# Gating the first weight loads on the second piece of x, with a new order of loads and new lists, in a fused attention and two-layer kernel

## The chip, the core and the metric

The kernel runs on one NeuronCore of a Trainium2 chip. The metric is the device time of one execution in microseconds (us); lower is better. Engines are named as in the profile: PE (TensorE, with PEld for its weight loads), DVE (VectorE), ACT (ScalarE), POOL (GpSimd) and SP (SyncE).

## The reference

Shapes: `x` is 8 batches x 8 heads x 512 tokens x 64, `state` is 8 x 8 x 32 x 64, `w_in` is 512 x 2048, `w_out` is 2048 x 512, `s` and `b` are single numbers. All are float32.

```python
# attention, per batch and head, scale = 1/8
a     = softmax(scale * x @ state.T)        # 512 x 32
xread = a @ state                           # 512 x 64
a2    = softmax(scale * state @ x.T)        # 32 x 512
sread = a2 @ x                              # 32 x 64
rows  = concat([xread, sread], axis=tokens) # 544 tokens a batch, 512 wide over the heads
# two layers on all 4352 rows
h = rows @ w_in
g = s * relu(h) ** 2 + b
out = g @ w_out
```

## The kernel before, in words

**Tiling.** The 512 tokens of a batch are one unit of work, and the eight batches go through the same steps. For a batch, `x` is transposed (`xT`), the scores of all heads come out as one tile of 128 partitions (8 heads x 32 states in two groups `g`) by 512 tokens (`T`, then `E` after the exponential, which also leaves the row sums for `sread`), and the softmax over the 32 states divides by column sums that a matmul with a block matrix of ones makes (`D`, then a logarithm and an exponential of its negative on ACT, then a product on DVE: `a4`). The read of the states and the first layer are folded together: `M[b, c] = state x w_in` for the quarter `c` of the 2048 columns (`part_M`, 8 small matmuls on quarters of the array), so that the first layer is `M.T @ a4` (`layer1`, 32 matmuls of 512 columns a batch, two groups accumulated). ACT takes the relu out of PSUM (line 996), DVE squares it (line 1002). The second layer of batch 0 is 64 plain matmuls of 512 columns (`layer2_first`); later batches use sums and differences of blocks (`pair_sums`, `weight_sums`, `layer2`) with 256 columns. The 32 rows of `sread` of all batches are done last (`layer1_slots`, `layer2("sr")`).

**PSUM.** There are three pairs of banks (`ps`, traced as `pair`) and two single banks (`ob`, traced as `o`). A product `M[b, c]` named in `APART` is written to two single banks, one per group, and copied by two instructions that may be on two engines; another is written to one pair and copied whole (batch 0's `c` of 0 and 1 by two copies out of the pair).

**The order of the work.** Every step is an `op` with its reads and writes. `TURNS` gives, for each engine, the numbers of its steps in the order in which that engine issues them; `Plan.order` merges the five lists and chooses buffers. An engine therefore never passes a step whose inputs are late: what stands behind it waits. In the first 20 us `Plan.order` also puts in matmuls on a tile of zeros (`fill`, traced as `warm`) where PE would otherwise sit idle; there are 59 of them.

**The loads at the start.** SP issues the four pieces of batch 0's `x` (`x0_load`, tile `xf`, traced as `u`, two heads of each half of the heads in each) and two tiny loads of `s` and `b`. ACT issues the identity and the first batch's states (`stf[0]`). GpSimd issues the loads that also turn float32 into float16: the quarters of `w_in` (`wi`, from 1 MB each to 512 KB), the quarters of `w_out` (`wo`) and the batches of `x` (`xn`). All of these wait for one small copy on GpSimd, the *gate* (line 552), which reads two columns of the identity, so no load of this queue is issued before the identity has landed. The order of GpSimd's loads is: gate, `wi0`, the states of batches 1 and 2 (`stf[1]`), `x` of batch 1, `wi1`, `wo0`, `wi2`, `wo1`, `wi3`, `wo2`, `wo3`, `x` of batch 2 and so on. A load that would be the ninth on its way waits for the one eight before it.

**The states.** `st_v` reads `state` with a state's 64 numbers (256 bytes) as one piece. `att_st(i)` casts them, each doubled, to `st16` (DVE), transposes them on PE with `is_transpose` into float16 in PSUM and copies them to `stT` (DVE).

Of the kernel before, what the change touches and what calls it, by code (L numbers as in the profile page):

```python
# [11 lines left out]
FP16 = mybir.dt.float16  # L12
# [6 lines left out]
        27 29 25 31 35 33 39 36 40 50 48 80-81 187 84-85 185 53 59 189 92-93 88-89 117 192 118 125-126 121  # L19
        113 122-123 127 119 68 70 114-115 124 116 128 193 120 96 141 129-130 99 237 131-133 225 74 134 142  # L20
        135 145 136 234 137 146 102 147 105 149 148 150-152 161-162 76 108 165-166 240 163 138 111 143
        167-168 164 243 139 222 144 72 62 157 140 158 153 159 56 228 154 160 231 173 155 174 1051 65 330 175
        156 169-171 267 333 258 334 259 268 260-263 269-270 172 176 271 264 272-274 348 351 1056 78 265 345
        354 360 286 277 287-289 694 445 278-281 290-291 282-284 339 357 292 342 293 295-299 454 567 1061
        305-306 300-301 307 302 308 696 576 452 309 315 310 316 311 317 312 318-322 570 572 1066 375-379 448
        689 450 384-387 380 476 388 381-382 467 479 464 389-390 394 482 395 461 391 470 396-397 403 398-401
        473 592 404-405 412 406-407 413-415 408-409 416 410 589 417-419 422 698 692 574 432-436 583 437
        423-424 438 425 439 426-428 586 429 604 601 506 497 507 711 595 498-499 508 598 509 500 510 501-504
        511-512 714 513 516-519 1071 1076 525-526 520-521 527 522-523 528 939 811 529-530 534 531-532
        535-541 544 820 932 935 554-556 545 557-561 546 720 723 619-621 726 622 547-549 705 550-551 623-626  # L30
        717 708 628-630 638-639 631-633 640 634-635 641-642 848 647 643 648-653 644-645 654 845 656-663 1086
        1081 937 941 666-668 676-677 669-670 814 816 818 671-672 678-680 673 954 681 836 741-744 682-683 830
        745-746 957 747 750 748 751-753 833 754-755 760 756 761-763 757 764-766 842 769-770 767 771-775
        778-781 776 782-785 839 788 798-799 789 800 790 801 827 969 963 791 802-805 951 960 1106 792 863 948
        864 793 865 794 866 795 867 1101 868-870 872-878 1091 882 879 883 966 884-888 891-892 1096 889
        893-898 900-906 910 907 911-915 920-921 916-917 1121 1111 984 922 1116 985-986 923 987 924-926
        988-989 927 990 1126 993 991 994-1000 1003-1010 1012-1019 1021-1028 1031-1035 1041 1036 1042
        1037-1038 1043-1048 1143-1150 1152-1159 1162-1169 1171-1178 1180-1187 1190-1197 1200-1207
    """,
    "ACT": """  # L40
        20-21 30 23 37 41 38 42 44 52 45 51 82 86 60 190-191 94 90 194-195 69 197-198 97 100 238 226 235 103
        106 77 109 241 244 223 63 57 229 232 67 331-332 335-336 349 352 79 346 361 355 695 447 446 340 358
# [4 lines left out]
    """,  # L47
    "DVE": """
        24 28 22 26 34 32 6 47 43 49 46 188 83 186 61 7 87 54-55 1057 91 71 95 196 199 98 75 1052 214 101
        239 210 104 215 206 236 107 207 227 110 252 112 218 209 179 177 64 73 245 58 219 242 224 1053 233 66  # L50
        220 230 246 216 253 325 337 183 208 181 247 1058 211 266 248 275 249 347 255 250 256-257 350 356 212
        217 213 285 221 1062 353 254 251 1067 294 341 457 1063 458 303 459 344 369 313 323 1068 363 370 364
        362 359 366 579 371 367 580 365 383 372 581 368 373 392 466 701 402 374 472 1072 484 463 478 469 411
        702 420 481 1077 485 703 475 491 440 585 430 494 594 488 495 492 489 486 588 487 606-608 713 505 597
        514 603 1078 496 493 616 524 940 490 533 1073 542 591 1082 610 936 562 823-824 600 825 944 552 613
        627 1087 617 722 611 945 614 719 636 609 946 728 716 646 615 612 655 707 618 1088 664 1083 942 725
        735 819 710 674 729 684 738 732-733 956 749 730 850 736 739 737 847 758 835 731 768 777 786 734 832
        838 854 740 841 860-861 844 971 959 806 829 855 857 1110 796 851 965 858 852 859 871 962 1105 880
        953 975 856 950 853 972 890 968 1108 899 1103 908 862 976-977 918 1100 981 1098 978 1118 973 1113
        982 928 983 992 979 1125 974 1001 1093 1120 980 1011 1128 1130 1095 1131 1020 1134 1123 1115 1135  # L60
        1029 1137 1140 1136 1138 1132 1141 1039 1049 1151 1160 1133 1142 1170 1139 1179 1188 1198 1208
    """,
    "POOL": """
        8-9 11 16 10 12-15 17-19 329 200 204 202 444 566 180 304 314 276 393 688 810 1060 421 441 182 431
        515 563 324 184 665 178 637 675 1065 1055 759 1070 1080 543 1075 1090 1085 807 685 909 881 919 553
        787 929 797
    """,
    "SP": """
        0-5 327 201 203 328 442 205 443 326 564 338 565 456 1059 687 686 578 460 1064 700 582 1054 704 930
        808-809 931 1079 822 943 1074 826 947 1084 1069 1089 1050 1040 1030 1161 1002 1189 1199 1209  # L70
# [16 lines left out]
class Plan:  # L87
# [60 lines left out]
    def order(self, fill):  # L148
# [3 lines left out]
        dma_free = {"sw": 7.05, "hw": 0.0}  # L152
# [5 lines left out]
        mode, out = "full", []  # L158
# [138 lines left out]
def kernel(  # L297
# [18 lines left out]
    P = 128  # L316
# [36 lines left out]
    APART = {(1, 0), (1, 1), (2, 0), (2, 1)}  # L353
# [40 lines left out]

    nc.vector.memset(warm, 0.0)
# [43 lines left out]
    def x0_load(i):  # L439
        op(  # L440
            {"SP": 0.5},
            lambda e: nc.sync.dma_start(xf_ap(i), x0_v[:, x0_heads(i)]),
            wr=[K(("xf", i))],
            dma=("hw", 0.75),
            lands=(3.6, 4.7, 6.0, 6.5)[i],
        )
# [25 lines left out]
    def wi_load(c):  # L472
        op(
            {"POOL": 0.85},
            lambda e: nc.gpsimd.dma_start(
                out=wi[c],
                in_=moe_w_in.rearrange("(k p) f -> p k f", p=P)[:, :, c * FC : c * FC + FC],
            ),
            rd=[g0],
            wr=[K(("wi", c))],  # L480
            dma=("sw", MB),
        )
# [61 lines left out]
    for i in range(4):  # L544
# [14 lines left out]
    op(  # L559
        {"POOL": 0.9},  # L560
# [858 lines left out]
```

## Time and profile before

| what | value |
|---|---|
| median of 3 runs | 208.2 us (207.3 to 208.93) |
| the profiled execution's own time | 208.01 us |
| its span, first to last instruction | 206.2 us |
| PE busy, PE matmuls | 199.3 us (97%), 1989 |
| DVE, ACT, POOL busy | 164.3, 109.3 and 38.8 us |
| granted clock of PE | 1.000 |
| HBM read, written | 17.33 MB, 8.91 MB |

The execution takes 1.8 us more than its span. A "busy" PE counts the zero-tile matmuls too, and overlapping matmuls are shown with more than their share (a 512-column matmul has 379 ns in its row, while the next one begins 216 ns later), so the work that PE has got done by a moment is counted in matmuls, not in busy time. `wi` and `wo` appear as sources by those names, the gate as `gate`, the identity as `ident`, the states as `stf`, `st` and `stT`.

### The profile page before, as it was taken

The numbers are of one execution on the slowest core, as the hardware profiler recorded it, in microseconds if no ns is written. First come the engines' busy times: TensorE is split into PE (matmuls) and PEld (weight loads), VectorE is DVE, ScalarE is ACT, GpSimd is POOL, SyncE is SP. The second block draws the span as 40 slices with busy tenths as digits, with TensorE's granted clock in tenths as the row PEclk, the third lists the DMA queues.
The fourth block names the chain that finished last, engine by engine and source line by source line (L and its number), as shares of the span: only waits on it lengthen the run. The fifth ranks groups of instructions, "written<-read, shape, count | busy, mean of one in ns | idle before, by whom it ended". The sixth has DMA issues, their size and how long they took to land.

```text
span 206.2 us, 4768 instructions
## 1 busy us (share of the span) xinstructions
PE 199.3 (97%) x1989; PEld 134.7 (65%) x1989; DVE 164.3 (80%) x325; ACT 109.3 (53%) x153; POOL 38.8 (19%) x60
## 2 busy tenths in 40 slices
PE   7979999999999999999999999999999999999992
PEld 3744444435666665677577767766776688888881
DVE  2327637989899979899999988997969689859871
ACT  4757786467588879468644473254606634130000
POOL 4832002001020120331301030033070200331000
PEclk9999999999999999999999999999999999999999
DMA  5999999992999992798991470233020200253054
GB/s 173 201 197 204 206 205 179 179 198 16 186 139 195 143 221 41 110 134 154 199 194 60 80 222 13 51 111 118 0 103 3 102 0 2 71 187 105 0 176 131
DMA packets 47285, 25.83 MB, mean 125 GB/s; under 512 B 31616, under 2 KB 45440, under 8 KB 47264
## 3 DMA queue, kind: packets, MB, share of 16 engines
q0 software_dynamic: 13792, 15.34, 38.0%
q1 hardware_dynamic: 33056, 10.10, 26.4%
q8 instruction: 15, 0.25, 0.5%
q10 hardware_dynamic: 416, 0.10, 0.2%
q14 instruction: 6, 0.05, 0.1%
HBM read 17.33 MB, written 8.91 MB: 127 GB/s over the span
## 4 chain that ended last, share of the span: by engine, by line
PE 89%; DMA 7%; DVE 1%; issue 0%; ACT 0%; POOL 0%; DVEq 0%
PE o L335 48%; PE pair L335 41%; DMA wi<-in_moe_w_in_dram 4%; DMA out_dram<-osb 2%; DMA ident<-ident_const 1%; DVE osb L1281 0%; DVE M L422 0%; ACT M L422 0%; DVE osb L1270 0%; DVE aN L906 0%; DVE sr L933 0%; POOL gate L552 0%; DVEq L1270 0%
## 5 line engine op out<-in xcount | busy, mean ns | idle before, releaser
L996 ACT ACTIVATE g<-pair 128x1024 f16<-128x1024 f32 x64 | 63.0, 1023 | 44.5 <-PE pair L335 44.4
L335 PE MATMUL pair<-a,M 128*128 128x512 f16 x256 | 63.3, 379 | 0.1
L335 PEld LDWEIGHTS <-pd 128*128 128x128 f16 x480 | 46.4, 98 | 10.1 <-issue 1.5
L335 PEld LDWEIGHTS <-g 128*128 128x128 f16 x424 | 40.7, 98 | 17.5 <-issue 2.9
L1002 DVE TENSOR_TENSOR g<-g 128x1024 f16<-128x1024 f16 x64 | 42.8, 683 | 2.8 <-ACT g L996 2.8
L335 PE MATMUL o<-u,pd 128*128 128x256 f16 x360 | 44.2, 273 | 0.0
L335 PE MATMUL o<-wo,g 128*128 128x256 f16 (+1 forms) x272 | 42.6, 285 | 0.0
L335 PEld LDWEIGHTS <-M 128*128 128x128 f16 x256 | 24.7, 98 | 22.9 <-DVE M L422 0.6
L1173 POOL DMA_DIRECT2D out_dram<-osb x28 | 18.8, 724 | 103.2 <-DVE osb L1281 54.5
L1270 DVE SCALAR_TENSOR_TENSOR osb<-o,s,bias_bc 128x512 f32<-128x512 f32 (+1 forms) x32 | 22.9, 715 | 7.3 <-PE o L335 5.7
L422 ACT CAST M<-pair 128x1024 f16<-128x1024 f32 (+1 forms) x22 | 20.4, 958 | 7.8 <-PE pair L335 7.8
L1281 DVE SCALAR_TENSOR_TENSOR osb<-o,s,osb 128x512 f32<-128x512 f32 (+1 forms) x24 | 17.2, 716 | 7.6 <-PE o L335 7.4
L1082 DVE TENSOR_TENSOR pd<-g 128x1024 f16<-128x1024 f16 (+1 forms) x32 | 20.7, 651 | 0.1
L335 PE MATMUL o<-wo,pd 128*128 128x256 f16 x120 | 19.0, 273 | 0.0
L335 PE MATMUL o<-u,g 128*128 128x256 f16 x120 | 17.5, 273 | 0.0
L422 DVE CAST M<-pair 128x1024 f16<-128x1024 f32 (+1 forms) x8 | 9.2, 1153 | 4.9 <-PE pair L335 3.8
L1093 DVE TENSOR_TENSOR pd<-g,pd 128x512 f16<-128x512 f16 (+1 forms) x32 | 12.5, 400 | 0.1
L1043 ACT ACTIVATE g<-pair 128x256 f16<-128x256 f32 x16 | 5.3, 385 | 13.0 <-PE pair L335 13.0
L1090 DVE TENSOR_TENSOR pd<-g,pd 128x512 f16<-128x512 f16 (+1 forms) x32 | 12.1, 400 | 0.1
L782 ACT ACTIVATE E<-pair 128x512 f16<-128x512 f32 x16 | 9.5, 600 | 4.7 <-issue 2.3
L335 PE MATMUL pair<-wi,stT 64*32 64x512 f16 x224 | 9.8, 383 | 1.5 <-DMA wi<-in_moe_w_in_dram 1.2
L463 POOL DMA_DIRECT2D xn<-in_x_dram x7 | 6.3, 909 | 25.2 <-ACT g L996 15.1
(70 smaller groups left out, 143.7 us busy)
## 6 DMA issues: line engine op xcount, KB each, us to landing
out_dram<-osb POOLq DMA_DIRECT2D x28, 256.0 KB, 3.2
xn<-in_x_dram POOLq DMA_DIRECT2D x7, 512.0 KB, 8.6
wi<-in_moe_w_in_dram POOLq DMA_DIRECT2D x4, 512.0 KB, 13.2
wo<-in_moe_w_out_dram POOLq DMA_DIRECT2D x4, 512.0 KB, 17.4
u<-in_x_dram SPq DMA_DIRECT2D x4, 256.0 KB, 3.9
out_dram<-osb SPq DMA_DIRECT2D x4, 256.0 KB, 2.7
out_dram<-osb SPq DMA_DIRECT2D x4, 128.0 KB, 2.3
pd<-in_state_dram SPq DMA_DIRECT2D x1, 320.0 KB, 4.0
```

The source lines that it names most:

```text
L335: return nc.tensor.matmul(out, lhsT, rhs, start=start, stop=stop, tile_position=tp, is_transpose=is_transpose, skip_group_check=True,)
L422: (nc.scalar.copy if e == "ACT" else nc.vector.tensor_copy)(dst, src)
L463: lambda e: nc.gpsimd.dma_start(out=T(xn[b]).rearrange("p h c d -> p h (c d)"), in_=x[b].rearrange("h (q c) d -> q h (c d)", q=P),),
L782: nc.scalar.activation(T(E[b])[:, g, :].rearrange("p (m t) -> p m t", m=2), T(u)[:, :, hS * g : hS * g + hS], AF.Exp, scale=scale, accum_o ...
L996: lambda e, u=u, part=part: nc.scalar.activation(part(), T(u), AF.Relu),
L1002: lambda e, part=part: nc.vector.tensor_mul(part(), part(), part()),
L1082: nc.vector.tensor_tensor(view()[:, :, 0:2], blocks(b, j)[:, :, 1:2, :].to_broadcast((P, 2, 2, n)), blocks(b, j)[:, :, 0:4:3, :], ALU.subt ...
L1090: nc.vector.tensor_tensor(view()[:, :, 2], blocks(b, j)[:, :, 3], view()[:, :, 0], ALU.subtract)
L1093: nc.vector.tensor_tensor(view()[:, :, 3], blocks(b, j)[:, :, 2], view()[:, :, 2], ALU.subtract)
L1173: lambda e: eng(e).dma_start(dst, src()),
L1270: lambda e: nc.vector.scalar_tensor_tensor(t_view(u), o_view(bank), s_bc, bias(h), ALU.mult, ALU.add),
L1281: lambda e: nc.vector.scalar_tensor_tensor(t_view(u), o_view(bank), s_bc, t_view(u), ALU.mult, ALU.add),
```

## The change

- The gate copy on GpSimd reads two columns of the second piece of batch 0's `x` (`xf(1)`) in place of the identity.
- The states are read in the order in which they lie in memory (`st_near`): 512 bytes a partition for batch 0, 1 KB a partition for batches 1 and 2. The transposing matmuls are plain ones with the identity as the moving operand, into float32 in PSUM, and write to strided columns so that `stT` comes out as before.
- The load of `stf[1]` leaves GpSimd's queue. SP issues it behind the six first loads, after a small new copy on DVE that reads `E[0]` of the second group and so holds it until batch 0's exponentials are done.
- Batch 0's `M[0, 1]`, `M[0, 2]` and `M[0, 3]` go to single banks (`APART`). `M[0, 0]` stays in a pair, and its second copy is made to wait for its first.
- The five lists are new. GpSimd's loads now run: gate, `wi0`, `wi2`, `wi3`, `wi1`, `wo0`, `x` of batch 1, `wo1`, `wo2`, `wo3`, `x` of batch 2. PE does all of batch 0's first layer ahead of its second layer and ahead of batch 1. Some constants that `Plan.order` uses to merge the lists are new.

```diff
-    APART = {(1, 0), (1, 1), (2, 0), (2, 1)}
+    APART = {(0, 1), (0, 2), (0, 3), (1, 0), (1, 1), (2, 0), (2, 1)}
...
+    def st_near(b0, b1):
+        rows = state[b0:b1].rearrange("b h j d -> (b h j) d")
+        return rows.rearrange("(q r) d -> q r d", q=P)
...
-    nc.scalar.dma_start(stf[0], st_v[:, 0:NG, :])
+    nc.scalar.dma_start(stf[0], st_near(0, 1))
...
-        lambda e: nc.gpsimd.tensor_copy(gate, ident16[:, 0:2]),
+        lambda e: nc.gpsimd.tensor_copy(gate, xf_ap(1)[:, 0, 0:2]),
+        rd=[K(("xf", 1))],
         wr=[K(("start",))],
-        since=2.85,
...
     wi_load(0)
     wi_load(1)
-    op(
-        {"POOL": 0.9},
-        lambda e: nc.gpsimd.dma_start(out=stf[1], in_=st_v[:, NG : NS * NG, :]),
-        rd=[g0],
-        wr=[K(("stf", 1))],
-        dma=("sw", 0.45),
-    )
     wo_load(0)
...
-            return T(u).rearrange("p a f -> p (a f)").bitcast(FP16).rearrange("p (n q) -> p n q", q=P)
+            return T(u)[:, 0, 0 : n * P]
...
                 mm(
-                    view()[:, k, :],
+                    view().rearrange("p (q r) -> p r q", r=n)[:, k],
                     st16[:, b0 * NG + k].rearrange("p k d -> p (k d)"),
                     ident16,
-                    is_transpose=True,
                 )
...
-            lambda e: copy(e, stT[:, b0 * NG : b1 * NG], view()[:, 0:n]),
+            lambda e: copy(e, stT[:, b0 * NG : b1 * NG].rearrange("p n q -> p (n q)"), view()),
...
-        if b == 0 and c < 2:
+        if b == 0:
             for g in range(NG):
                 op(
                     {"ACT": 0.48, "DVE": 0.64},
                     lambda e, g=g: copy(e, T(M[b, c])[:, g], T(u)[:, g]),
-                    rd=[K(u)],
+                    rd=[K(u)] + [K(M[b, c], 0)] * g,
...
     att_scores(0)
+    op(
+        {"DVE": 0.08},
+        lambda e: nc.vector.tensor_copy(stf[1][:, 0, 0:2], T(E[0])[:, 1, 0:2]),
+        rd=[K(E[0], 1)],
+        wr=[K(("stf", 1))],
+    )
+    op(
+        {"SP": 0.5},
+        lambda e: nc.sync.dma_start(out=stf[1], in_=st_near(1, NS)),
+        wr=[K(("stf", 1))],
+        dma=("hw", 0.4),
+        lands=16.6,
+    )
     att_st(1)
```

More of the change, by code (lines that the diff above doesn't have):

```diff
@@ L24 @@
[L24 to L28, printed above, removed]
@@ new lines @@
+        125 129 126 121 188 190 119 130 122 131 123 72 192 136-137 132 138 133 144 134 195 145 196 135 139
+        152-153 127 154-155 140 148-150 79 111 168-169 246 151 164-165 114 166-167 170-171 240 237 54 146
+        243 141 63 225 142 228 143 156 147 74 57 160 234 161 231 162-163 157 66 333 176-178 158 179 159 336
+        270 172 337 1054 173 271 261-262 174 272 175 273 263-265 274 266 345 267 342 351 354 1059 268 348
+        275-276 357 81 448 280-281 277 282-286 289 287 290-293 697 699 579 294-295 298-299 363 360 300-301
@@ new lines @@
+        369 356 367 582 375 583 372 584 386 1075 370 368 1080 1071 484 373 395 371 481 376 472 704 377 405
+        374 414 705 469 423 475 478 706 597 487 466 443 494 433 491 497 488-489 600 594 495 603 498 492 508
+        616 591 617 490 517 606 1076 527 618 493 536 1081 609 545 499 613 588 496 610-611 826 555 612 719
+        716 565 827-828 614 630 619 1090 725 620 735 731 639 710 649 947 658 722 948 1085 667 621 615 713
+        1091 738 949 1086 732 728 677 941 739 733 736 835 850 687 737 741 838 752 742 761 853 771 740 832
@@ L444, in x0_load @@
             dma=("hw", 0.75),
-            lands=(3.6, 4.7, 6.0, 6.5)[i],
+            lands=(3.75, 4.7, 5.95, 6.25)[i],
         )
@@ L480, in wi_load @@
             wr=[K(("wi", c))],
-            dma=("sw", MB),
+            dma=("sw", MB + 0.44 * (c == 3)),
         )
@@ L604, in att_st @@
             wr=[key],
-            since=(5.0, 0.0, 0.0)[i],
+            since=(4.1, 0.0, 0.0)[i],
         )
@@ L621, in att_st @@
         op(
-            {"DVE": 0.1 + 0.07 * n},
-            lambda e: copy(e, stT[:, b0 * NG : b1 * NG], view()[:, 0:n]),
+            {"DVE": 0.07 + 0.135 * n},
+            lambda e: copy(e, stT[:, b0 * NG : b1 * NG].rearrange("p n q -> p (n q)"), view()),
             rd=[K(u)],
```

67 lines of the change are left out of this document (31 added, 36 removed), and 8 rows, old and new, of the table TURNS.

## The prediction

> **What bounds the kernel now.** I read the page first, then the windows by stage, then the chain that ended last, then the order of time of the first 24 us.
>
> ```profile
> span 206.2 us, 4768 instructions
> PE 199.3 (97%) x1989; PEld 134.7 (65%) x1989; DVE 164.3 (80%) x325; ACT 109.3 (53%) x153; POOL 38.8 (19%) x60
> ```
>
> ```profile
> core 0: us, PE busy (x) PEld busy (x) DVE busy (x) ACT busy (x) POOL busy (x), PEclk, DMA share, GB/s
> 6.00:11.70 5.70, 4.51 (x55) 3.20 (x52) 1.50 (x5) 4.14 (x9) 3.80 (x5) 1.00 1.19 182
> 11.70:20.00 8.30, 8.13 (x94) 4.60 (x94) 4.88 (x11) 5.37 (x10) 3.37 (x4) 1.00 1.25 204
> 20.00:23.05 3.05, 3.05 (x15) 1.27 (x13) 1.96 (x4) 3.01 (x4) 0.00 (x0) 1.00 1.24 207
> 23.05:202.20 179.15, 178.85 (x1804) 122.88 (x1803) 153.94 (x294) 94.24 (x128) 28.73 (x43) 1.00 0.60 117
> ```
>
> From 23.05 to 202.20 PE has 0.3 us without work, at a full clock, and the program does not change the real matmuls. The end therefore moves with the moment at which PE has got through a given amount of real work, and that is decided in the first 23 us. There the chain runs through a load:
>
> ```profile
> 0.75 2.48 DMA ident<-ident_const
> ...
> 3.41 8.27 DMA wi<-in_moe_w_in_dram
> 11.68 0.04 issue
> 11.72 0.41 PE pair L335 x8
> ...
> 84.77 0.86 PE pair L335 x4
> ```
>
> The identity lands at 3.23, `wi0` is issued 0.18 us later and takes 8.27 us; only then does the first product `M` start. The last row gives the price of a 512-column matmul, 0.86 / 4 = 0.216 us.
>
> I take the moment 23.05 as a marker: 22.83 plus one matmul, in the rows below. Between 11.72 and there PE did 16 matmuls of the first layer, ten of the second and one for `D` (27 x 0.216 = 5.83 us), three products `M` at 0.22 (two take 23.14 to 23.69 with the change of mode), 20 transposes and batch 1's scores (some 1.3): 7.8 us of work in 11.3. In the new list the same 7.8 us are done when batch 0's whole first layer (32 x 0.216 = 6.9) and its four products (0.9) are done, just before the first matmul on `wo`. So the question is when that is.
>
> ```profile
> 22.83 0.38 PE L335 MATMUL o<-wo,g 128*128 128x512 f16 x1
> 23.14 0.63 PE L335 MATMUL pair<-wi,stT 64*32 64x512 f16 x16
> 23.69 0.76 PEld L335 LDWEIGHTS <-g 128*128 128x128 f16 x5 [0.42 <-issue]
> 4.81 0.62 ACT L422 CAST xn<-u 128x512 f16<-128x512 f32 x1 [0.22 <-DMA u<-in_x_dram]
> 6.76 0.62 ACT L422 CAST xn<-u 128x512 f16<-128x512 f32 x1
> 9.01 0.79 POOL L475 DMA_DIRECT2D wi<-in_moe_w_in_dram  x1
> 12.09 0.43 DVE L422 CAST st<-stf 128x512 f16<-128x512 f32 x1 [3.34 <-DMA stf<-in_state_dram]
> 12.43 0.42 DVE L829 TENSOR_TENSOR a<-E,a 128x512 f16<-128x512 f16 x1
> 13.26 0.42 DVE L422 COPY stT<-pair 128x512 f16<-128x512 f16 x1 [0.41 <-PE pair L335]
> 14.89 1.02 ACT L996 ACTIVATE g<-pair 128x1024 f16<-128x1024 f32 x1 [1.13 <-PE pair L335]
> 15.12 0.89 POOL L463 DMA_DIRECT2D xn<-in_x_dram  x1 [1.55 <-DMA xn<-in_x_dram]
> 17.73 0.87 POOL L463 DMA_DIRECT2D xn<-in_x_dram  x1 [1.73 <-DMA wi<-in_moe_w_in_dram]
> 18.00 0.59 ACT L422 CAST M<-pair 128x512 f16<-128x512 f32 x1 [0.57 <-PE pair L335]
> 18.61 0.69 DVE L422 CAST M<-pair 128x512 f16<-128x512 f32 x1 [1.08 <-ACT M L422]
> 23.91 1.23 DVE L422 CAST M<-pair 128x1024 f16<-128x1024 f32 x1 [1.24 <-PE pair L335]
> ```
>
> **The gate.** The second piece of `x` ends an idle stretch of ACT at 4.81, so it lands by 4.79; with the 0.18 above, `wi0` is issued at 4.97 and not at 3.41, 1.56 us later. All ten loads of GpSimd's first burst stand behind it. How long `wi0` then takes has two rows as its ends.
>
> ```profile
> wi<-in_moe_w_in_dram POOLq DMA_DIRECT2D x1, 512.0 KB, 8.3
> ...
> xn<-in_x_dram POOLq DMA_DIRECT2D x1, 512.0 KB, 5.7
> ...
> stf<-in_state_dram POOLq DMA_DIRECT2D x1, 128.0 KB, 7.8
> ```
>
> The first is `wi0` itself, issued while `x` is still on its way. The second, from the window 48 to 50, is a load of the same size issued into an empty queue. Lack of bandwidth doesn't explain the 8.3: from 6.00 to 11.70 the engines moved 182 GB/s x 5.7 us = 1,037 KB, while `wi0`, `stf[1]` and a last piece of `x` are about 920 KB. Later loads were already moving while a share of `wi0` was still out. With the new gate, `x`'s last piece (in use at 6.76 before) is all but down when `wi0`'s first bytes can move, so the empty queue is the nearer row: `wi0` lands at 4.97 + 5.7 = 10.7, with 13.25 (4.97 + 8.27) as the upper end. Before it was 11.68.
>
> The Trainium skill's page "DMA: Bandwidth & Descriptors", section "Anatomy of one DMA — SWDGE (gpsimd) path", puts a load at 2.0 us plus its bytes over 436 GB/s, an estimate of 4.4 us for the 1 MB that is read here, or 9.4 for the landing. The trace does not agree: its empty-queue load took 5.7. With 9.4 the marker below would still be held at 22.0 by ACT.
>
> **The new order of loads.** In the loaded stretch one load follows another at 2.6 us (`x` of batch 1 releases GpSimd at 15.12, `wi1` at 17.73). `stf[1]`, which came 0.4 us behind `wi0` (12.09 against 11.72), now moves beside `wi3`; I charge 0.4 there. Landings: `wi0` 10.7, `wi2` 13.3, `wi3` 16.3, `wi1` 18.9, `wo0` 21.5, `x` of batch 1 24.1.
>
> **Batch 0's scores.** Their chain no longer waits for DVE's cast at 12.09. From `x`'s last piece to the last product `a4` it is a cast, transposes, copies, scores, two exponentials with sums, two logarithms, two exponentials of 0.6 each on ACT and a product of 0.42; counted on from 6.3 to 6.76 it ends at 13.6 to 14.0, beside `M[0,0]` (10.7 + 0.45 product + 0.2 + two copies of 0.69 with a 0.42 between them = 12.5 for the first use, 13.6 for the second). The two meet, so neither gains from the other being earlier.
>
> **Single banks and the first layer.** `M[0,2]`, `M[0,3]` and `M[0,1]` are each copied in halves, 0.59 on ACT beside 0.69 on DVE, in place of one copy of 1.23: about 0.5 us sooner behind its load. Now the walk. First matmuls 12.7; with `wi2` at 13.3 batch 0's first two blocks are through by 14.6 and the third by 15.6. From 14.8 ACT is the pace: two relus (1.02 each) to 16.8, the half of `M[0,3]` when `wi3` allows it, 17.0 to 17.6, three relus to 20.6, the half of `M[0,1]` to 21.2. Only then can PE do the last two 0.43 blocks: **marker at 22.4**. By the loads alone it would be about the same: `wi1` 18.9 + 0.45 + 0.2 + 0.7, then six 0.43 blocks. `wo0` (21.5), `x` (24.1, asked for at 24.6 behind nine matmuls) and the later weights then come ahead of their use.
>
> **The rest.** Two more changes of mode on PE lie behind the marker (44 against 42 by the lists), each 0.09 (23.14 less 23.05): +0.2. Float32 in PSUM makes the copies to `stT` dearer, at most 0.69 against 0.42 each; DVE is busy 1.96 of 3.05 us around the second, and has 25 us spare later, so nothing; without that cover it costs 0.5. The transposes stay six matmuls. The 1 KB packets save time on a load that nothing waits for now. The added copy on DVE holds back `M[0,0]`'s copy only if the exponentials end behind 11.3; the nearest row of two elements is under 0.1 us. Behind SP's held load stands `x` of batch 2's transpose, issued at 35 in the old trace; free.
>
> **The sum.** 22.4 - 23.05 + 0.2 = -0.45: a span of 205.7 and, with the 1.8 us that the profiled execution (208.01) has beside its span, **207.5 us**. That execution lies 0.2 under the median of 208.2.
>
> **The rivals.**
>
> *The first weights stay late.* If the 8.27 us belong to GpSimd's own burst (its eighth issue begins at 9.01, and `wi0` lands 1.9 us after that issue ends) and not to `x`, then the later gate moves everything: `wi0` 13.25, `wi1` 21.5, the four last blocks behind it end at 24.5, and the span is 206.2 + 1.45 + 0.2 = 207.9: **209.7 us**, slower. It decides from `wi0` landing after 11.5. For it: the bytes were moving, only a share of `wi0` was not. Against: the empty-queue row, and that each later load came at the steady 2.6. The skill's same page, section "Latency and other measured facts", says that two of the sixteen DMA engines are usually slower on GpSimd's loads, with port contention by its descriptors as a guess; the bytes above agree with a straggler, no row shows which engine it was.
>
> *The states of batches 1 and 2 come late.* SP issues them at about 10.5, into a queue full of weights. By the nearest row (7.8) they land at 18.3; the cast on DVE (line 598's step) stands ahead of the squares and of the first half of `M[0,1]`, which can start at 19.6. Up to there it is free, beyond it each us costs one. Should the load get through only behind the seven loads already issued, at about 26.5, the marker goes to 29: **some 214 us**. Against: `x` and `stf[0]`, from two queues, shared the engines well.
>
> *It gains more than I say.* The queues kept apart bring `x` down sooner and `wi0` at 10.0, ACT's chain then holds the marker at 21.9, and the new lists lose the 0.3 us of idle time behind 23.05: -1.15 + 0.2 - 0.3: **206.8 us**. For it: ACT has 3.01 of 3.05 us busy before the marker, so it is the next bound in both; against: another list has as likely more holes as fewer.
>
> **How the numbers follow.** Forecast 0.55, its own range 206.7 to 208.4 (marker 21.9 to 22.9, and 0.4 either way for holes). Late weights 0.20, late states 0.10, larger gain 0.15. A measurement of this kernel tells about 1% from no change (the three runs lie within 0.8%): that is below 206.1 or above 210.3. The scatter of the runs may take half of the last rival and a little of the forecast below 206.1: 0.13. Above 210.3 lie the late states and half of the late weights: 0.20. The rest, 0.67, is within 1%. The range takes in the late weights and the larger gain: 206.0 to 210.2.
>
> **What would show it.** Right: the gate's copy ends about 4.9, `wi0` is waited for until 10.5 to 10.9, the next three products follow at 13.3, 16.3 and 18.9, ACT has almost no idle time from 15 to 21, the first `wo,g` matmul starts near 22.4, and PE is without holes from there to 4 us before the end. Wrong: `wi0` beyond 11.5 (first rival), DVE idle on `stf` beyond 19.6 (second), or PE idle in the stretch behind the marker by a microsecond or more, which no row of before can price.

## The result, and the profile after

The changed kernel takes 209.03 us (median of 20 runs, 208.32 to 209.47) against 208.22 us for the kernel before in the same session: a ratio of 1.0043, 95% interval 1.0027 to 1.0059. Repeated later (run `after2`) it was 1.0062, interval 1.0041 to 1.0084. So the change makes the kernel slower by about half a per cent. 207.5 us was forecast, a small gain, so the direction was wrong; the time lies within the forecast's range of 206.0 to 210.2.

The page of the changed kernel begins with its span and busy times, to be held against 206.2 us and 199.3 us of PE before:

```profile
span 206.9 us, 4781 instructions
PE 200.0 (97%) x1989; PEld 134.9 (65%) x1989; DVE 162.4 (79%) x325; ACT 111.2 (54%) x156; POOL 37.1 (18%) x59
```

The order of time of its first 24 us (start, duration, engine, line, operation, count, and in brackets the idle time before it and what ended it):

```profile
4.94 0.18 POOL L556 CAST gate<-u 128x2 f16<-128x2 f32 x1 [4.49 <-DMA u<-in_x_dram]
5.06 3.26 POOL L479 DMA_DIRECT2D wi<-in_moe_w_in_dram  x4
10.70 0.41 PE L335 MATMUL pair<-wi,stT 64*32 64x512 f16 x8 [0.21 <-DMA wi<-in_moe_w_in_dram]
13.41 0.41 PE L335 MATMUL o<-wi,stT 64*32 64x512 f16 x8
14.83 1.94 ACT L992 ACTIVATE g<-pair 128x1024 f16<-128x1024 f32 x2 [0.36 <-PE pair L335]
17.12 0.41 PE L335 MATMUL o<-wi,stT 64*32 64x512 f16 x8 [0.70 <-DMA wi<-in_moe_w_in_dram]
17.62 0.58 ACT L426 CAST M<-o 128x512 f16<-128x512 f32 x1 [0.85 <-PE o L335]
18.10 2.86 ACT L992 ACTIVATE g<-pair 128x1024 f16<-128x1024 f32 x3
19.70 0.41 PE L335 MATMUL o<-wi,stT 64*32 64x512 f16 x8
20.82 0.62 ACT L426 CAST M<-o 128x512 f16<-128x512 f32 x1
22.73 0.59 PE L335 MATMUL pair<-wo,g 128*128 128x512 f16 x2
```

The first product is where it was forecast (10.70). The third is 0.8 us late: `wi3` landed at 17.07, 3.7 us behind `wi2`. PE waits 0.70 for it and ACT 0.85 for the product, and the fourth product (19.70) and the marker, the first `wo,g`, are 0.8 and 0.3 us later than forecast. ACT has no idle time from its copy at 17.62 to the end of the one at 20.82. Against the recorded execution of before, 22.73 is still 0.32 better than 23.05.

Behind the marker the changed kernel is slower. The window from each marker to PE's end, for the changed kernel (before: 179.15 us, 178.85 busy):

```profile
22.73:202.89 180.16, 179.54 (x1827) 123.15 (x1825) 152.39 (x295) 96.76 (x134) 28.80 (x44) 1.00 0.64 117
```

That is 1.01 us more than in the recorded execution of before: 0.62 idle in place of 0.30 by the trace, and 0.69 more of busy time at the same granted clock. The idle time is one stop at 52, which the order of time shows:

```profile
51.17 0.42 DVE L1086 TENSOR_TENSOR pd<-g,pd 128x512 f16<-128x512 f16 x1
51.70 0.75 DVE L1209 SCALAR_TENSOR_TENSOR osb<-pair,s,bias_bc 128x512 f32<-128x512 f32 x1
52.50 0.38 PE L335 MATMUL pair<-wo,g 128*128 128x512 f16 x1 [0.62 <-DVE osb L1209]
```

In the new DVE list the copy of an out tile from a pair stands directly ahead of the matmul that needs that pair.

### The profile page after: what moved, and what is told of

It is laid out like the page before. It is cut to its first block, busy times and chain, and to the rows that moved or that the text cites. A ratio compares the mean times of both kernels' runs of the same rounds, so it can differ in the third digit from the quotient of the medians.

```text
span 206.9 us, 4781 instructions
## 1 busy us (share of the span) xinstructions
PE 200.0 (97%) x1989; PEld 134.9 (65%) x1989; DVE 162.4 (79%) x325; ACT 111.2 (54%) x156; POOL 37.1 (18%) x59
## 4 chain that ended last, share of the span: by engine, by line
PE 89%; DMA 7%; POOL 1%; DVE 1%; SPq 0%; issue 0%
PE o L335 49%; PE pair L335 40%; DMA wi<-in_moe_w_in_dram 5%; DMA u<-in_x_dram 2%; POOL wi L479 1%; DVE osb L1209 0%; DVE osb L1266 0%; SPq L446 0%; POOL gate L556 0%
## 5 line engine op out<-in xcount | busy, mean ns | idle before, releaser
L335 PE MATMUL o<-wo,g 128*128 128x256 f16 (+1 forms) x272 | 42.1, 285 | 0.0
L1169 POOL DMA_DIRECT2D out_dram<-osb x28 | 19.6, 763 | 83.1 <-DVE osb L1277 71.4
L426 ACT CAST M<-pair 128x1024 f16<-128x1024 f32 x21 | 20.6, 1014 | 10.5 <-PE pair L335 10.5
L335 PE MATMUL o<-wo,pd 128*128 128x256 f16 x120 | 17.7, 273 | 0.0
L946 POOL COPY srd<-srdT 128x128 f16<-128x128 f16 x8 | 7.0, 1098 | 21.4 <-DMA srdT<-sr 21.4
L335 PE MATMUL pair<-wo,g 128*128 128x512 f16 x32 | 10.2, 380 | 0.6 <-DVE osb L1209 0.6
```

The source lines that it names most:

```text
L335: return nc.tensor.matmul(out, lhsT, rhs, start=start, stop=stop, tile_position=tp, is_transpose=is_transpose, skip_group_check=True,)
L426: (nc.scalar.copy if e == "ACT" else nc.vector.tensor_copy)(dst, src)
L946: lambda e: nc.gpsimd.tensor_copy(srd[:, :, :, b], srdT[:, b]),
L1169: lambda e: eng(e).dma_start(dst, src()),
```

## The experiments

Ratios are to the kernel before, measured in the same session, with 95% intervals. "First `wo,g`" is the start of the first matmul on `wo`; in the list of before it stands 2.38 us ahead of the marker (20.67 and 23.05 in the recorded execution, and the same matmuls follow it at the same distance in all others), in the new list it is the marker.

### The gate alone, and the changed kernel without it (`b_gate`, `a_ident`)

```diff
 # b_gate: the kernel before with
-        lambda e: nc.gpsimd.tensor_copy(gate, ident16[:, 0:2]),
+        lambda e: nc.gpsimd.tensor_copy(gate, xf_ap(1)[:, 0, 0:2]),
+        rd=[K(("xf", 1))],
         wr=[K(("start",))],
-        since=2.85,
 # a_ident: the changed kernel with the same lines the other way round
```

> The kernel before with the gate alone changed (second piece of x in place of the identity); lists and all else as before. Theory 1 (the gate brings the first weights down sooner, because the loads of x and of the weights no longer overlap; the loss of the whole change lies elsewhere): the first piece of w_in lands at about 10.7 us instead of 11.7, everything up to 23 us moves by that, about 207.3 us against 208.2 (ratio 0.995 to 0.997). Theory 2 (the later gate is what costs): the piece lands at 12.5 or later, 209 to 210 us (ratio 1.004 or more).

> The changed kernel with the gate put back on the identity; everything else as changed. Theory 1: one share of the weights straggles again, the first piece lands at about 11.7 instead of 10.66 and the other three follow as late, so about 210.0 us against the changed kernel's 209.0 (ratio to the kernel before 1.007 to 1.010), with a wider scatter from run to run. Theory 2: the loads start 1.6 us sooner and land sooner, 207.5 to 208.5 us (ratio 1.000 or less).

Measured: `b_gate` 1.0033 (1.0013 to 1.0054; 208.27 against 207.53 us), `a_ident` 1.0025 (1.0005 to 1.0045). The gate alone makes the old kernel slower. With the identity's gate the ratio of the new one falls from 1.0043 to 1.0025, which points the same way, though the two intervals overlap. The first theory, in which the gate gains and everything is lost behind the marker, falls. What made it plausible was one number: `wi0` at 11.68 in the recorded execution of before.

### Is 11.68 the habit of the kernel before? (`before2`, `before3`, `before4`)

The same kernel, unchanged.

> The kernel before once more, unchanged, for a second look at its head. Theory 1 (wi0's landing at 11.68 in the first profile was one late execution and not the habit of the kernel; with the identity's gate wi0 usually lands at about 10.9, as in the run of the changed kernel with that gate, 10.85): wi0 10.6 to 11.2, PE idle of at most 0.6 us before its first product, span 205.4 to 205.9, ratio 1.000. Theory 2 (11.68 is what this gate gives, and the gate on the second piece of x gains a microsecond there): wi0 11.5 to 11.9, span 206.1 to 206.4.

> A look at the head of the kernel before. Theory 1 (the early landing is the habit): wi0 at 9.0 to 9.7, the second layer-one weight at 16.0 to 16.5, span 205.0 to 205.5. Rival (the late one is as frequent): wi0 at 11.4 to 11.9, the second at 17.2 to 17.6, span 206.0 to 206.4.

> As the last: theory 1, wi0 at 9.0 to 9.7 and a span of 205.0 to 205.5; rival, wi0 at 11.4 to 11.9 and 206.0 to 206.4.

The ratio of `before2` to the other runs of the same kernel was 1.000 (0.9976 to 1.0023). The order of time of `before2` and then of `before3`, PE's first product, a later one for `wi1`, and the first `wo,g`:

```profile
10.61 0.41 PE L335 MATMUL pair<-wi,stT 64*32 64x512 f16 x8
16.30 0.41 PE L335 MATMUL pair<-wi,stT 64*32 64x512 f16 x8
19.45 0.38 PE L335 MATMUL o<-wo,g 128*128 128x512 f16 x1
```

```profile
11.34 0.41 PE L335 MATMUL pair<-wi,stT 64*32 64x512 f16 x8 [0.49 <-DMA wi<-in_moe_w_in_dram]
17.93 0.41 PE L335 MATMUL pair<-wi,stT 64*32 64x512 f16 x8
21.09 0.38 PE L335 MATMUL o<-wo,g 128*128 128x512 f16 x1
```

In `before2` nothing waits for `wi0` (no bracket): it had landed at 9.42. With `b_sr` and `b_sr2` (below; their head is that of before) there are six executions:

| execution | `wi0` issued | `wi0` landed | `wi1` landed | first `wo,g` |
|---|---|---|---|---|
| recorded before | 3.41 | 11.68 | 17.45 | 20.67 |
| `before2` | 2.90 | 9.42 | 16.26 | 19.45 |
| `before3` | 3.84 | 11.30 | 17.82 | 21.09 |
| `before4` | 3.38 | 11.94 | 17.67 | 20.90 |
| `b_sr` | 2.83 | 9.06 | 16.20 | 19.46 |
| `b_sr2` | 3.35 | 9.98 | 16.50 | 19.69 |

Neither the early nor the late landing is the habit: three are early, three late, by the means 2.2 us apart at `wi0` and 1.3 at `wi1`, and the identity itself came anywhere from 2.7 to 3.7. The mean of first `wo,g` is 20.21, a marker of 22.59, not 23.05. Theory 1, as put in these expectations (the late one is an exception), falls too; its rival, that the late one is as frequent, holds, though `before3` lies outside its figures (`wi1` at 17.82, a span of 207.2).

The view of the DMA queues tells the two kinds apart. These are the rows of GpSimd's queue from the start to the landing of `wi0`, of the recorded execution of before and of `before2` (packets, MB, share):

```profile
q0 software_dynamic: 1298, 1.03, 59.5%
q0 software_dynamic: 743, 0.74, 47.4%
```

`wi0` itself is 0.52 MB. In the three late executions 0.90 to 1.05 MB had gone through the queue by then, in the three early ones 0.73 to 0.77: a landing is late where bytes of later loads go ahead of the last of `wi0`, as the prediction had read it. Why an execution is of one kind or the other is open.

### Does the later gate only give up the early kind? (`b_gate_l2`, `b_gate_l3`, `b_gate_l4`, and a later gate, `b_gate3`)

`b_gate` again, three times, and the kernel before with the gate on the fourth and last piece of `x`:

```diff
 # b_gate3, against b_gate
-        lambda e: nc.gpsimd.tensor_copy(gate, xf_ap(1)[:, 0, 0:2]),
-        rd=[K(("xf", 1))],
+        lambda e: nc.gpsimd.tensor_copy(gate, xf_ap(3)[:, 0, 0:2]),
+        rd=[K(("xf", 3))],
```

> Theory (the later gate gives up the early landings and keeps the rest: half of the executions lose 1.2 us, the other half nothing, 0.6 on the mean, as measured 0.69): wi0 at 10.3 to 11.2, the second layer-one weight at 17.2 to 17.8, first wo,g matmul at 20.4 to 21.0. Rival (the landings scatter with this gate too, and the loss lies elsewhere): the second layer-one weight at 16.2 to 16.6 in about half of the looks, first wo,g matmul at 19.4 to 19.8.

> As the last. Theory: the second layer-one weight at 17.2 to 17.8. Rival: at 16.2 to 16.6 in about half of the looks.

> As the last. Theory: the second layer-one weight at 17.2 to 17.8. Rival: at 16.2 to 16.6 in about half of the looks.

> The kernel before with GpSimd's gate on the fourth and last piece of x, so that the first weight is issued at about 6.3 instead of 2.9 to 3.4 (4.7 with the second piece). Theory 1 (GpSimd's loads share one rate of about 205 KB per us behind their start, and the marker follows the landing of the second layer-one weight by 3.2 us, so what the start loses beyond x's own traffic is lost at the end): wi0 at 12.0 to 12.6, the second layer-one weight at 18.6 to 19.2, first wo,g matmul at 21.8 to 22.4, ratio 1.007 to 1.012. Rival (the start does not matter, x and the weights need the same bytes in any order; the 0.33% of the gate on the second piece was chance): ratio 0.999 to 1.004.

`b_gate3`: 1.0114 (1.0088 to 1.014); `wi0` 12.28, `wi1` 19.14, first `wo,g` 22.42, as its first theory had it. The four executions of `b_gate` have `wi1` at 17.43, 17.43, 18.19 and 17.87, and first `wo,g` at 20.62, 20.62, 21.38 and 21.06: none early, the last two beyond what was expected. Their mean first `wo,g`, 20.92, is that of the three late executions of before, 20.89; the three early ones have 19.53. So the theory holds in the main: the later gate gives up the early kind and keeps the rest. The chain that ended last in `b_gate` shows what is waited for (start, duration, what):

```profile
6.37 0.88 POOL xn L463
7.25 10.18 DMA wi<-in_moe_w_in_dram
17.43 0.04 issue
17.47 0.45 PE pair L335 x8
```

The order of time of `b_gate3`:

```profile
6.28 0.19 POOL L552 CAST gate<-u 128x2 f16<-128x2 f32 x1 [5.83 <-DMA u<-in_x_dram]
19.26 0.41 PE L335 MATMUL pair<-wi,stT 64*32 64x512 f16 x8
22.42 0.38 PE L335 MATMUL o<-wo,g 128*128 128x512 f16 x1
```

In all eleven executions with the old list, first `wo,g` starts 3.2 to 3.3 us behind the landing of `wi1`. From `b_gate` to `b_gate3` the issue moves by 1.69 us (4.71 to 6.40) and `wi1` by 1.71, and the ratios 1.0033 and 1.0114 are 1.7 us apart; against the means of the four executions of `b_gate` it is 1.5 (4.90 to 6.40) and 1.4 (17.73 to 19.14). Beyond the second piece of `x`, a later start is lost nearly whole. From the identity to the second piece the mean of first `wo,g` moves by 0.71 (20.21 to 20.92), and the medians of that session by 0.74 (207.53 to 208.27). The sign and size of the gate in the old list are thereby settled. The windows from 4 to 8 us show what it gives up. Rows of the recorded before, of `before2`, `b_gate`, the changed kernel and `a_ident`, in that order; the last column is GB/s:

```profile
4.00:8.00 4.00, 3.93 (x46) 2.98 (x45) 1.38 (x5) 2.89 (x5) 4.00 (x6) 1.00 1.10 238
```

```profile
4.00:8.00 4.00, 3.85 (x45) 3.08 (x44) 1.69 (x4) 2.54 (x5) 4.00 (x6) 1.00 1.14 248
```

```profile
4.00:8.00 4.00, 4.00 (x47) 3.32 (x46) 1.52 (x5) 2.40 (x5) 3.41 (x6) 1.00 0.79 177
```

```profile
4.00:8.00 4.00, 4.00 (x42) 3.50 (x41) 1.74 (x6) 1.70 (x3) 3.06 (x5) 1.00 0.63 167
```

```profile
4.00:8.00 4.00, 4.00 (x29) 3.31 (x28) 1.65 (x4) 1.45 (x3) 4.00 (x6) 1.00 1.08 235
```

With the identity's gate the transfers of `x` run out into those of the weights; with the later gate some 60 to 70 GB/s are not moved for four microseconds, up to 280 KB, between `x`'s last bytes and the weights' first. From 8 to 20 us these five executions move 179 to 217 GB/s. At 205 KB per us the gap is worth 1.3 us, and 0.7 arrives at the last weight of the new list. Part of it is got back because fewer bytes of later loads go ahead: by the landing of that weight GpSimd's queue has moved 2.37 MB in the changed kernel (19.57) and 2.50 in `a_ident` (18.91).

The gap is not all of it. The recorded before has none (238 GB/s), and its `wi1` lands at 17.45, as late as that of `b_gate` (17.43). What the later gate gives in return is an orderly first landing: in all ten executions with a gate on `x`, `wi0` lands 5.5 to 6.0 us after its issue, with 0.63 to 0.73 MB through the queue. What is won by this and what is lost by the later start are about even against a late execution of before; against an early one only the loss is left.

### The stop at 52, the states' load, and both with the other gate (`a_hole`, `a_early`, `after2`, `a_idhole`, `a_idholet`)

```diff
 # a_hole, in DVE's list of the changed kernel: the copy of the pair's other bank (186) later, directly ahead of 184
-        236 1065 255 210 256 186 340 1056 245 184 257-258
+        236 1065 255 210 256 340 1056 245 186 184 257-258
 # a_early: the states of batches 1 and 2 loaded at 4.1, not held to batch 0's exponentials
-        lambda e: nc.vector.tensor_copy(stf[1][:, 0, 0:2], T(E[0])[:, 1, 0:2]),
+        lambda e: nc.vector.tensor_copy(hold, T(E[0])[:, 1, 0:2]),
-        wr=[K(("stf", 1))],
+        wr=[K(("hold",))],
 ...
-        lands=16.6,
+        lands=7.5,
 # a_idhole: a_hole and the gate on the identity. after2: the changed kernel again.
 # a_idholet: a_idhole, and the state transposed in the transposing form
-            return T(u)[:, 0, 0 : n * P]
+            return T(u).rearrange("p a f -> p (a f)").bitcast(FP16).rearrange("p (n q) -> p n q", q=P)
-                    view().rearrange("p (q r) -> p r q", r=n)[:, k],
+                    view()[:, k, :],
+                    is_transpose=True,
-            lambda e: copy(e, stT[:, b0 * NG : b1 * NG].rearrange("p n q -> p (n q)"), view()),
+            lambda e: copy(e, stT[:, b0 * NG : b1 * NG]
+                .rearrange("p n q -> p (n q)").rearrange("p (q r) -> p r q", r=n), view()[:, 0:n]),
```

> The changed kernel with one step moved on DVE: the copy of batch 0's fourth output bank (which stands ahead of the last matmuls into the third bank of the same pair) is put directly ahead of the copy of the third. Theory 1 (PE's 0.8 us stop at 51.6 us is a wait of those matmuls for that copy, and is lost time): the stop goes, 208.3 us (ratio to the kernel before 1.000 to 1.001). Theory 2 (DVE or ACT is as far behind at that point, so the stop only moves): a stop of 0.5 us or more within the next 10 us, 208.9 to 209.1 us (ratio 1.003 to 1.0045).

> The changed kernel with the load of batches 1 and 2's states issued by SP right behind its six first loads, at about 4.1 us (the copy on DVE that held it back until batch 0's exponentials now writes another tile). Theory 1 (that load, falling between the pieces of w_in, makes the third of them 1.1 us late and everything behind it): the third piece lands 2.6 us behind the second, the first wo,g matmul starts at 21.9 instead of 22.73, 208.2 us (ratio 0.999 to 1.001). Theory 2 (the lateness is the fetch of code at 14.3 us, or ACT sets the pace anyway): the third piece still 3.4 us or more behind, or the matmul at 22.5 or later, 208.8 to 209.2 us (ratio 1.003 to 1.005).

> The changed kernel once more, unchanged, beside the next two. Both theories: ratio to before 1.0035 to 1.005. In its profile wi0 at 10.5 to 10.8, wi3 3.3 to 3.8 behind wi2, x of batch 1 at 24.6 to 25.1, the stop of PE at about 51.6 in front of a pair (0.79 us over the usual distance of two matmuls) there again.

> The changed kernel with the gate back on the identity and the copy of bank 3 of the first out pair one place later in DVE's list (behind the copy of bank 2 alone). Theory 1 (the later gate costs 0.5 us before the marker, the stop at 51.6 costs 0.6 behind it, and the two add): first wo,g matmul at 22.2 to 22.4, no stop at 51.6, span 205.5 to 206.0, 1.0 us under the changed kernel: ratio to before 0.999 to 1.0015. Theory 2 (the gate is worth nothing in ordinary runs, only the place behind the marker counts): as the run with the list alone, 1.003 to 1.004.

> As the last, and the state's six transposes again in the transposing form into contiguous 16-bit columns, the copy to stT putting the columns in order as it writes. Theory 1 with the transposes as a third term (0.109 us each as plain matmuls into strided columns, 0.055 in the other form): 0.2 to 0.3 under the last run, its profile with six transposes at about 0.055; ratio 0.9985 to 1.0005. Rival (the transposes stand in slack of PE before the marker and cost nothing): equal to the last run within 0.1 us.

| run | ratio (95%) | last layer-one weight | first `wo,g` | span |
|---|---|---|---|---|
| changed kernel | 1.0043 (1.0027 to 1.0059) | 19.57 | 22.73 | 206.9 |
| `after2` | 1.0062 (1.0041 to 1.0084) | 20.03 | 23.09 | 207.2 |
| `a_hole` | 1.0038 (1.002 to 1.0057) | 19.70 | 22.81 | 206.3 |
| `a_early` | 1.0043 (1.0018 to 1.0067) | 18.99 | 22.36 | 207.6 |
| `a_ident` | 1.0025 (1.0005 to 1.0045) | 18.91 | 22.25 | 206.4 |
| `a_idhole` | 1.0019 (1.0 to 1.0037) | 18.88 | 22.15 | 206.1 |
| `a_idholet` | 1.001 (0.9987 to 1.0034) | 19.36 | 22.52 | 206.0 |

`after2` was somewhat slower than expected, with `wi0` at 11.13. `a_early` lies between its two theories in its rows (`wi3` 3.2 us behind `wi2`), `a_idhole` between those of its own in its ratio.

**The gate in the new list.** The three executions with the gate of the change and the late states have their last layer-one weight at 19.77 on the mean, the three with the identity at 19.05, and their first `wo,g` at 22.88 and 22.31: 0.57 us for the gate, without overlap, and 0.4 to 0.8 us between the medians' ratios.

**The stop.** In `a_hole` it is gone, in the order of time of PE:

```profile
51.57 0.38 PE L335 MATMUL o<-wo,g 128*128 128x256 f16 x2
51.79 0.38 PE L335 MATMUL pair<-wo,g 128*128 128x512 f16 x1
```

From the marker to PE's end it takes 179.53 us. The changed kernel, `after2` and `a_ident`, which all have the stop with 0.62 us, take 180.16, 180.15 and 180.15: in the profiled executions the stop is lost whole. In the medians the gain is not resolved: 1.0038 lies inside the interval of the changed kernel, and the ratio is that of the second theory, though the later stop which that theory asks for isn't there. The same edit with the other gate (1.0025 to 1.0019) isn't resolved either; there most of it is given back by a stop further on (180.02 us in `a_idhole`). The rows are of `a_idhole`, then of `a_early`:

```profile
103.19 1.04 PE L335 MATMUL pair<-a,M 128*128 128x512 f16 x4 [0.32 <-DMA a<-aN]
```

```profile
104.64 0.39 PE L335 MATMUL pair<-a,M 128*128 128x512 f16 x1 [0.94 <-DMA a<-aN]
```

The changed kernel comes to this place at 103.92 and `a_hole` at 103.36, both without a wait, so a PE that is further ahead meets it. That doesn't explain `a_early`, whose wait ends at 104.64. `a_early` has its last weight 0.6 to 1.0 earlier and its marker 0.4 to 0.7 earlier, and its profiled execution loses more than that here; its ratio is no better, as its second theory had it.

**The transposes.** The four state transposes behind the marker, in the order of time of `a_ident` (plain matmuls into float32) and of `a_idholet` (transposing form into float16):

```profile
23.33 0.60 PE L335 MATMUL pair<-ident,st 128*128 128x128 f16 x4
```

```profile
23.60 0.39 PE L335 MATMUL pair<-ident,st 128*128 128x128 f16 x4
```

0.21 us on PE at this place, as expected of theory 1. It doesn't reach the end in the trace: from the marker to PE's end `a_idholet` takes 179.52 us, as `a_hole` does (179.53), since a matmul at 103.06 comes late by what was won. The ratio falls by 0.0009, which is within the intervals. The Trainium skill's page "Perfetto Trace Analysis", section "Transposes", asks for the transposing form in place of a plain matmul; these rows agree, though here the type and the stride of the output changed with it.

### All together, and the stop of the old list (`a_best`, `a_bestx`, `b_sr`, `b_sr2`)

`a_best` is `a_idholet` with the early states and DVE's product `aN` of batch 5 two places earlier; `a_bestx` is the same with the gate on the second piece of `x`. `b_sr` (and `b_sr2`, the same kernel) is the kernel before with two neighbours of DVE's list exchanged.

```diff
 # a_best, against a_idholet, beside the lines of a_early
-        374 414 705 469 423 475 478 706 597
+        374 414 705 469 423 706 475 478 597
 # b_sr, against before
-        457 1063 458 303 459 344 369 313 323 1068 363
+        457 1063 458 303 459 344 369 313 1068 323 363
```

> The changed kernel with the gate on the identity, the copy of bank 3 one place later, the transposing form for the state, the states of batches 1 and 2 loaded by SP at 4.1 instead of 10.4, and DVE's product aN of batch 5 two places earlier (ahead of two squares), so that its transposing load starts 1.2 us sooner than the matmul at 103 needs it. Theory 1 (the terms add: 0.6 us of landing from the early states, 0.3 from the wait at 103): fourth layer-one weight at 18.2 to 18.9, first wo,g matmul at 21.4 to 22.1, no wait for the transposed a, span 204.6 to 205.5, ratio 0.995 to 0.9985. Rival (the next load or list takes it back): ratio 0.9995 to 1.001 as the last run without the two edits.

> The same with the gate on the second piece of x, as in the change. Theory 1 (the gate alone costs 0.4 to 0.7 us, whatever stands around it): ratio 0.002 to 0.0035 above the last run; wi0 no earlier than 10.4, the fourth layer-one weight 0.3 to 0.8 later than there. Rival (with the states out of the way the gate is worth nothing, the loss came only with the states' load in the middle of the weights): equal to the last run within 0.001.

> The kernel before with two neighbours in DVE's list exchanged: the product sr of batch 2 ahead of the copy of an out piece that waits for its buffer's store (the stop of PE at 75 us). It is a third look at the head of before too. Theory 1 (a stop of PE behind the marker is lost whole unless a later wait takes it back): no stop at 75, 0.45 us less, ratio 0.997 to 0.999; wi0 anywhere from 9.4 to 11.7, as the two looks so far. Rival (PE then waits later, as the changed kernel without its stop at 51.6 did at 103): ratio 0.9995 to 1.001.

> The run b_sr once more. Theory 1 (a stop of PE behind the marker that no later wait takes back is lost whole): 0.45 us less than before, ratio 0.997 to 0.999. Rival (given back later): 0.9995 to 1.001.

`a_best` 1.0022 (1.0 to 1.0045), `a_bestx` 1.0021 (0.9999 to 1.0042): theory 1 missed in both, and 1.001 at most, the rival's figure for `a_best`, is within the interval. For `a_bestx` the rival holds: with the states' load out of the weights' way no cost of the gate is left, within the 0.4 us or so that the intervals allow. In `a_best` the last layer-one weight lands at 19.07; PE had a granted clock of 0.56 in that execution, so only its weight loads, which wait for no work of PE, are used. In `a_bestx` it lands at 19.08, level with that and with the kernels with the identity's gate, and the window from 4 to 8 us is fuller than with the later gate before:

```profile
4.00:8.00 4.00, 4.00 (x39) 3.50 (x38) 1.55 (x5) 1.29 (x3) 3.12 (x5) 1.00 0.76 192
```

So what the gate costs in the new list is the unused transfer time ahead of the weights together with the states' load in their midst; the early states use that gap. But no time is won over `a_idholet`. The stop at 103 is still there, though `aN` moved its load forward; SP's issue and PE's wait in `a_bestx`:

```profile
94.63 1.23 SPq L918 DMA_TRANSPOSE a<-aN  x1
103.05 1.04 PE L335 MATMUL pair<-a,M 128*128 128x512 f16 x4 [0.20 <-DMA a<-aN]
```

In `a_idhole` that load was issued at 95.85 and the matmul began at 103.19. The issue is 1.2 us earlier and the wait ends 0.14 earlier, so DVE's `aN` does not set it. What does is open.

`b_sr`: 0.9989 (0.9967 to 1.001), `b_sr2`: 0.9983 (0.9955 to 1.0011). The order of time of DVE in `b_sr` shows the exchange, `sr` now ahead of the copy that waits for its buffer:

```profile
73.26 0.29 DVE L933 TENSOR_TENSOR sr<-pair,rs 128x128 f16<-128x128 f32 x1 [0.97 <-issue]
73.47 0.74 DVE L1270 SCALAR_TENSOR_TENSOR osb<-o,s,bias_bc 128x512 f32<-128x512 f32 x1
```

PE then has no wait behind the first `wo,g` that the view of waits lists. From the marker to PE's end the two executions take 178.78 and 178.84 us, the four of the unchanged kernel 179.12, 179.33, 179.69 and 178.96, with a stop at this place of 0.27, 0.47, 0.84 and at most 0.1. Both runs point to 0.1 to 0.2%, neither interval leaves out 1. It is the fastest version found and the only one whose medians lie below the kernel before.

## Why the prediction was wrong, point by point

**What bounds the kernel: right.** The end moves with the marker and with PE's stops behind it. In the old list first `wo,g` follows `wi1` by 3.2 to 3.3 us. In the new list the marker starts 5.11 to 5.12 us behind ACT's copy of its half of `M[0,3]` in all seven executions of the table and in `a_bestx`, while its distance from the last weight's landing varies from 3.1 to 3.4: behind that copy ACT sets the pace, as the walk had it.

**The gate: the landing was right, what it was compared with was not.** 4.97 and 10.7 were forecast, 5.06 and 10.66 came. The first step that failed is "Before it was 11.68", and with it the 23.05 that the sum subtracts. That was one execution of a kernel whose `wi0` lands between 9.06 and 11.94. Against the mean marker of six executions, 22.59, the changed kernel's mean of 22.88 (`a_hole` included, which has its head) is 0.3 worse; the sum had 0.65 better. That the late `wi0` of before is a matter of `x`'s competition, as the argument with the empty queue had it, is refuted as a rule: three executions landed it in 6.2 to 6.6 us with `x` still on its way. What holds of it is that with the gate on `x` the landing took 5.5 to 6.0 us every time. And the argument looked at `wi0` alone. Transfers that don't start while `x` runs out leave a gap in the windows from 4 to 8 us, and the later loads come behind it.

**The pace of the loads: mis-sized.** `wi3` was put 3.0 us behind `wi2`; it came 3.7 behind in both profiles of the changed kernel (4.1 in `a_hole`). With the early states it is 3.2 to 3.3, with the identity's gate 2.9 to 3.1, with both (`a_best`) 2.5. So the charge of 0.4 for the states was about right, and the rest of the excess came with the gate. It reached the marker through ACT, which was idle for 0.85 us ahead of `M[0,3]` and began its copy at 17.62, where 17.0 was forecast.

**ACT's chain: right, and a little shorter than put.** From that copy to the marker 5.4 us (17.0 to 22.4) had been allowed and 5.1 came, so a copy 0.6 late made the marker 0.3 late. The two sums that the prediction gives for 22.4 don't come out there: 21.2 and two blocks of 0.43 are 22.1, and 18.9 with 0.45, 0.2, 0.7 and six blocks is 22.8. The single banks and the 1 KB packets were not tried by themselves.

**The states.** DVE's cast at 18.27 didn't wait, so the rival of late states did not come about; nor did that of late first weights, whose point of decision, `wi0` beyond 11.5, wasn't reached. Slower came by a way that no rival had.

**Behind the marker: +0.2 was put, +0.9 came.** In the four executions of the unchanged kernel it is 178.96 to 179.69 us from the marker to PE's end, 179.27 on the mean; in the changed kernel, `after2` and `a_ident` 180.15 to 180.16. That is 0.88 more, and 1.01 against the recorded execution alone. "PE is without holes" failed by a stop of 0.62 in every one of these three; the old list's own stop is 0.4 on the mean. A new list did have a hole of its own, and the rival that let it gain here had the wrong sign. The busy time is 0.69 more. "The transposes stay six matmuls" held for the count, not for the time: 0.21 us of them lie behind the marker. Batch 1's transposes and scores, put at "some 1.3", take 1.62 in the changed kernel (23.81 to 24.21, 25.33 to 26.22 and 27.62 to 27.95), 0.1 more than these 0.21 explain. With the 0.2 for the changes of mode, as forecast and not measured alone, these make 0.5; 0.2 is not assigned.

**The sum put right:** the forecast was -0.45 us. The base was 0.46 too high (23.05 for 22.59), the marker 0.48 too early (22.4 for 22.88), the term behind it 0.68 too small (0.2 for 0.88). That gives +1.17; measured, by the medians, were +0.81 and +1.18. Each of the three alone uses up the gain that was forecast. Undoing gate, stop and transposes brings 1.0043 to 1.0062 down to 1.001. The gate is the one of the three whose effect stands outside the intervals by itself, and that in the old list. The stop's 0.6 us is the same in every profiled execution that has it, but no median shows it by itself; the transposes' 0.2 us is given back by the stop at 103 in `a_idholet` and `a_bestx`.

## What to carry to other kernels

A stall that one profiled execution shows at a load is a draw from a spread, and a change that is worth a few tenths of a microsecond there must be priced against several executions: the mean of six executions of the kernel before turns the sign of this forecast's head. A gate that keeps weights out of the way of the input can make the first landing orderly and still lose, because it starts every load of its queue later; look at the GB/s just behind the input, and fill a dip there with a load that is needed anyway, as the early states did here. And when PE gets ahead, look for the next thing that it meets.

## What the runs showed of the hardware

The same program had its first 512 KB load by GpSimd landed between 9.06 and 11.94 us, with 6.2 to 8.6 us from issue to landing; three executions were near 9.5 and three near 11.6, in runs on the same chip too (`before3` and `before4` late, `b_sr2` early). The issue explains only a part: 3.35 led to 9.98, and 3.38 to 11.94. In the new order of loads, with the identity's gate and an issue at 2.90 to 3.06, three executions gave 10.82 to 11.31 and none an early one; 0.94 to 0.98 MB had gone through GpSimd's queue by then, as in the late kind. Why the old order can be early and the new one was not is open. With the queue held back until a piece of `x` was down, ten executions took 5.5 to 6.0 us from issue to landing. In the stretch from 16 to 20 us all these kernels move 194 to 207 GB/s, whatever the order of their loads.
